# Two matrix products of a fused attention and MLP kernel rewritten as seven block products for eight

## The chip, the cores and the metric

The kernel runs on one core of a Trainium2 chip. A core has TensorE (PE in the profile; PEld are its weight loads), VectorE (DVE), ScalarE (ACT), GpSimd (POOL) and SyncE (SP, which issues most transfers). The metric is the device time of one execution in microseconds; the profile's span runs from the first to the last instruction.

## The reference, cut to what matters

```python
# attention: 2 batches, 12 heads, 448 tokens, head size 64, causal
scores = scale * np.matmul(q, k.transpose(0, 1, 3, 2))
scores = np.where(mask, -1000000000.0, scores)
scores = scores - np.max(scores, axis=-1, keepdims=True)
attn = np.exp(scores)
attn = attn / (np.sum(attn, axis=-1, keepdims=True) + 1e-09)
x = np.matmul(attn, v)            # as 896 tokens x 768
# first MLP: w_in 768 x 2048, w_out 2048 x 768
r = np.maximum(x @ w_in, 0.0)
x = (r * r) @ w_out
# second MLP: w1, w2, w3, w_o 768 x 768
h = np.maximum(np.maximum(x @ w1, x @ w2), x @ w3)
out = h @ w_o
```

q, k and v are float32, the weights arrive as float64 (the loads take them as four int16 a number).

## The kernel before, in words

Every engine runs its instructions in the order in which the function writes them (`manual_schedule`); semaphores hold an instruction until its operands are there.

**Attention.** Heads go in pairs (12 pairs, `Pair`). A pair has seven score units: `s` (TensorE, L246), `m` (VectorE: mask, minimum and a copy to SBUF, L257), `e` (ScalarE: exponential with its sum, L266), `r` (VectorE: reciprocal, L273, L274), `n` (GpSimd: multiply, L278), `g` (TensorE: transposes, L286), `h` (copies out of PSUM, L310, group 0 on VectorE, the others on ScalarE), `w` (TensorE: times v, L319), and `xh`, `xl`: the result of the pair split into a high part (ScalarE, `act_hi`, L128) and the rest (VectorE, `dve_lo`, L131). `ORDER` is a list, written out, of all these steps with the pair's number behind the point. It also has some first products of w_in (`p`, `a`, `b`), which fill TensorE.

**Products.** Each float32 product is three passes of TensorE: high x high, high x low, low x high. A weight block of 768 x 128 goes through five steps: `load` (SyncE queue, two buffers), `cast` (ScalarE, L159), `join` (VectorE, L166), `high_part` (ScalarE), `low_part` (VectorE). `decode` puts the steps of the next blocks and the evacuation of the last accumulators in turn. For w_in, `group` (L356) multiplies a block with both batches of x, 6 contraction blocks x 3 passes x 2 batches of 448 columns; then relu on ScalarE (L382), the product of relu and value on VectorE (L386), and the split into gh and gl. w_out takes 16 contraction blocks for each of 6 output blocks. w1, w2 and w3 run as w_in does, with maxima on VectorE (L586).

**Last product.** The product with w_o (L615) is already made from seven block products for eight, 384 columns each; its sums are made on VectorE (L553) and its results leave through L683 and L684.

Of the kernel before, what the change touches and what calls it, by code (L numbers as in the profile page):

```python
# [60 lines left out]
def tile_attention_moe_moe(  # L61
# [23 lines left out]


# [40 lines left out]
    def act_hi(hi, src):  # L127
        nc.scalar.copy(hi, src)  # L128

    def dve_lo(lo, src, hi):  # L130
        nc.vector.tensor_tensor(out=lo, in0=src, in1=hi.bitcast(F32), op=ALU.subtract)  # L131


    class Weight:

        def __init__(self, pool, w, k0, nk, c0, n, tag, bufs=None):
            self.pool, self.src, self.tag, self.bufs = pool, w, tag, bufs  # L140
# [606 lines left out]
```

## Time and profile before

| | |
|---|---|
| runs | 492.59, 492.68, 494.93 us (median 492.68) |
| profiled execution | 493.42 us, its span 491.5 us |
| TensorE busy | 486.4 us, 2587 matmuls |
| VectorE busy | 254.5 us, 530 instructions |
| ScalarE busy | 231.5 us, 451 instructions |
| GpSimd busy | 45.4 us, 99 instructions |
| granted TensorE clock | 1.00 throughout |

A busy share is an average over stages with different limits, and a matmul's end is modelled in the records, so neighbouring matmuls overlap. What a stage is limited by is read from the chain of waits and from the busy time of each engine in that stretch.

### The profile page before, as it was taken

The page shows a single profiled execution, that of the slowest core. Times are in us where ns is not written, and L with a number is a line of the kernel's source. Part 1 is how long each engine was busy: PE and PEld are TensorE (multiplying, and loading weights), DVE is VectorE, ACT ScalarE, POOL GpSimd, SP SyncE. Part 2 cuts the span into 40 slices and gives each one's busy share as a digit, 9 for nine tenths or more (in the row PEclk, how much of TensorE's full clock was granted, in tenths as well). Part 3 has the DMA queues.
Part 4 walks back from the last instruction along what each step waited for, and adds up shares of the span by engine and source line. Part 5 has one row for each costly group of instructions (what it writes and reads, how often), then busy time and mean ns, then how long its engine had stood idle before and what let it go on. Part 6 is the DMA issues. An engine that isn't in the chain of part 4 may idle for free.

```text
span 491.5 us, 6744 instructions
## 1 busy us (share of the span) xinstructions
PE 486.4 (99%) x2587; PEld 429.5 (87%) x2587; DVE 254.5 (52%) x530; ACT 231.5 (47%) x451; POOL 45.4 (9%) x99
## 2 busy tenths in 40 slices
PE   9999999999999999999999999999999999999997
PEld 5666667999999999999999999999999999999996
DVE  5877766555455456514315224226463638564942
ACT  6999996555455455414214224133443515332800
POOL 5655633000000000000000000000000000000000
PEclk9999999999999999999999999999999999999999
DMA  6553414252442441525225144133454435210022
GB/s 203 165 192 119 148 45 125 75 176 77 126 124 75 125 128 49 165 65 171 83 89 162 43 139 132 61 128 122 136 167 153 144 116 191 74 56 1 32 99 94
DMA packets 47615, 56.26 MB, mean 114 GB/s; under 512 B 1760, under 2 KB 43872, under 8 KB 47584
## 3 DMA queue, kind: packets, MB, share of 16 engines
q1 hardware_dynamic: 47296, 55.61, 35.6%
q8 instruction: 20, 0.33, 0.3%
q10 hardware_dynamic: 288, 0.23, 0.1%
q14 instruction: 11, 0.09, 0.1%
HBM read 53.08 MB, written 2.75 MB: 114 GB/s over the span
## 4 chain that ended last, share of the span: by engine, by line
PE 98%; DVE 1%; POOL 1%; issue 0%
PE ps L356 75%; PE ps L615 8%; PE ps L246 6%; PE ps L286 4%; PE ps L319 4%; POOL pr L278 1%; PE ps L465 1%; DVE pr L257 0%; DVE xl L131 0%; DVE wd L683 0%; DVE warm L463 0%; DVE st L273 0%; DVE st L274 0%; DVE st L257 0%
## 5 line engine op out<-in xcount | busy, mean ns | idle before, releaser
L128 ACT CAST wh<-wd 128x768 fp32r<-128x768 f32 (+1 forms) x52 | 42.2, 811 | 62.9 <-DVE wd L166 62.9
L159 ACT CAST up<-wr 128x768 f16<-128x768 bf16 (+1 forms) x58 | 60.7, 1046 | 9.8 <-DMA wr<-in_moe_w_out 5.0
L131 DVE TENSOR_TENSOR wl<-wd,wh 128x768 fp32r<-128x768 f32 (+1 forms) x52 | 48.1, 925 | 29.8 <-ACT wh L128 29.8
L356 PE MATMUL ps<-yh,wh 128*128 128x448 f32 x216 | 61.6, 366 | 0.0
L356 PE MATMUL ps<-yh,wl 128*128 128x448 f32 x216 | 61.6, 366 | 0.0
L356 PE MATMUL ps<-yl,wh 128*128 128x448 f32 x216 | 61.5, 366 | 0.0
L166 DVE SCALAR_TENSOR_TENSOR wd<-wr,up 128x768 int32<-128x768 int32 (+1 forms) x58 | 53.9, 929 | 9.1 <-ACT up L159 9.0
L356 PE MATMUL ps<-xh,wh 128*128 128x448 f32 x192 | 55.9, 367 | 0.0
L356 PE MATMUL ps<-xh,wl 128*128 128x448 f32 x192 | 55.7, 366 | 0.0
L356 PE MATMUL ps<-xl,wh 128*128 128x448 f32 x192 | 55.7, 366 | 0.0
L356 PE MATMUL ps<-gl,wh 128*128 128x448 f32 x192 | 54.5, 365 | 0.0
L356 PE MATMUL ps<-gh,wh 128*128 128x448 f32 x192 | 54.5, 365 | 0.0
L356 PE MATMUL ps<-gh,wl 128*128 128x448 f32 x192 | 54.5, 365 | 0.0
L266 ACT ACTIVATE pr<-pr,st 128x128 f32<-128x128 f32 (+3 forms) x84 | 44.0, 528 | 6.5 <-DVE st L257 6.5
L278 POOL TENSOR_SCALAR pr<-pr,st 128x128 f32<-128x128 f32 (+3 forms) x84 | 41.6, 513 | 32.2 <-DVE st L274 13.5
L386 DVE SCALAR_TENSOR_TENSOR r<-ps,r 128x448 f32<-128x448 f32 x32 | 18.6, 620 | 49.6 <-ACT r L382 49.6
L356 PEld LDWEIGHTS ps<-yl,wh 128*128 128x128 f32 x216 | 40.6, 188 | 3.5
L356 PEld LDWEIGHTS ps<-yh,wl 128*128 128x128 f32 x216 | 40.6, 188 | 3.5
L356 PEld LDWEIGHTS ps<-yh,wh 128*128 128x128 f32 x216 | 40.6, 188 | 3.5
L257 DVE CUSTOM_DVE_ANT_0 pr<-ps,mask 128x128 f32<-128x128 f32 (+3 forms) x84 | 34.5, 449 | 10.3 <-PE ps L246 9.4
L356 PEld LDWEIGHTS ps<-xl,wh 128*128 128x128 f32 x192 | 36.1, 188 | 3.1
L356 PEld LDWEIGHTS ps<-xh,wl 128*128 128x128 f32 x192 | 36.1, 188 | 3.1
(123 smaller groups left out, 620.5 us busy)
## 6 DMA issues: line engine op xcount, KB each, us to landing
wr<-in_moe_w_out SPq DMA_DIRECT2D x18, 768.0 KB, 4.3
wr<-in_moe_w SPq DMA_DIRECT2D x18, 768.0 KB, 4.3
wr<-in_moe_w_in SPq DMA_DIRECT2D x16, 768.0 KB, 4.7
v<-in_v SPq DMA_DIRECT2D x12, 256.0 KB, 3.4
wr<-in_moe_w_out SPq DMA_DIRECT2D x6, 512.0 KB, 3.7
q<-in_q SPq DMA_DIRECT2D x11, 256.0 KB, 2.9
k<-in_k SPq DMA_DIRECT2D x11, 224.0 KB, 3.7
out<-wd SPq DMA_DIRECT2D x9, 192.0 KB, 1.8
```

The lines of the kernel that those rows point to most:

```text
L128: nc.scalar.copy(hi, src)
L131: nc.vector.tensor_tensor(out=lo, in0=src, in1=hi.bitcast(F32), op=ALU.subtract)
L159: nc.scalar.copy(self.up.bitcast(FH)[:, :, 1::2], self.top)
L166: nc.vector.scalar_tensor_tensor(out=self.t.bitcast(I32), in0=self.rest, scalar=13, in1=self.up.bitcast(I32), op0=ALU.logical_shift_right, ...
L246: nc.tensor.matmul(sc[:, :keys[w]], self.n["q"][r, w // 2 * P:(w // 2 + 1) * P], self.n["k"][r, :keys[w]], start=True, stop=True,)
L257: nc.vector.tensor_tensor_reduce(out=self.pr[:, offs[u]:offs[u] + n], in0=self.sc[u][:, :n], in1=mask[:, mask.shape[1] - n:], scale=-SCALE ...
L266: nc.scalar.activation(sl, sl, ACTF.Exp, bias=self.st[:, 0, u:u + 1], scale=-1.0, accum_out=self.st[:, 1, u:u + 1],)
L278: nc.gpsimd.tensor_scalar(sl, sl, self.st[:, 2, u:u + 1], 1.0, op0=ALU.mult, op1=ALU.mult)
L286: nc.tensor.transpose(pt[:, i], self.pr[:, offs[u] + kc * P:offs[u] + (kc + 1) * P], shared["ident"])
L319: nc.tensor.matmul(self.pv[r, kc * P:], self.n["v"][:, kc, r], self.ph[:, h, at], start=kc == 0, stop=kc == NK - 1,)
L356: nc.tensor.matmul(acc[i], ww[:, cs], xx[:, tk], start=first and a == 0 and n == 0, stop=last and a == len(kcs) - 1 and n == 2,)
L615: nc.tensor.matmul(acc, x, w, start=start and a == 0 and i == 0, stop=stop and a == len(parts) - 1 and i == 2, skip_group_check=more,)
```

## The change

The products with w_in and with w1 to w3 are made from quarters. Of x (896 tokens x 768) a11 is batch 0 with the first three contraction blocks, a12 batch 0 with the last three, a21 and a22 the same of batch 1. Of two column blocks of a weight, each is cut into halves of three contraction blocks. Seven products M1 to M7 of sums of quarters take the place of eight. The sums of x are s3 = a11 - a21, s2 = a22 - s3, s1 = s2 + a11 and s4 = a12 - s2; they are made per contraction block on VectorE and each is split into high and low parts. The sums of weights are four subtractions on VectorE per pair of column blocks. M1, M6, M7 and M4 accumulate in one PSUM bank, and what it holds after M1, M6 and M7 is copied out by ScalarE (`keep`) and added on VectorE to the other two banks.

The head pairs are taken in the order that gives the four quarters of one contraction block together: pair i has batch i%2 and heads i//4 + 3*(i%4//2). `ORDER` is new, and steps of different pairs are interleaved singly. It holds four products (slots 0 to 3, steps `u`), their weight work (`k0` to `k26`) and the sums of x (`d`, `1h` to `4l`). Each later product is a slot; behind its matmuls stand the evacuation of the slot before, the weight work planned for it (`plan`, `LEAD` = 3 slots ahead) and extras, such as the conversion of g to gh and gl. SBUF is handed out as 47 equal units (`Units`). GpSimd's clearing of two `up` tiles becomes VectorE's of one, put first. w_out and the last product keep their number of matmuls; the last one's sums and conversions are spread over the end of the w1 to w3 stage and its own.

```diff
-FILL, EARLY = 1, 2
+LEAD = 3
+RING = 5
+OWN, MORE = 29, 18
+BESIDE = 4
 ORDER = """
...
+w3.9 k14 r2.11 n2.11 h0'.10 e5.11 h2.10 u0.2 d3.9 h1.10 k16 k17 u1.0 n3.11 e6.11 g1.11 n0.11 w0.10
+r0.11 k23 w1.10 n6.11 3h.9 k20 2l.7 n1.11 w2.10 w3.10 h1.11 u3.0 u1.1 k18 n4.11 xf.10 xh.10 k19
+n5.11 g2.11 g0.11 k21 xl.10 h2.11 h0'.11 g3.11 u1.2 h3.11 v1.0 w0.11 k24 w1.11 k25 k26 w2.11 w3.11
+d2.11 2h.11 d4.11 d1.11 4h.11 2l.11 u3.1 xh.11 4l.11 1h.11 1l.11 xl.11 u2.1 u3.2 3l.9 u2.2 v2.0
...
+    class Quarter:
...
+        def hi(self):
+            self.t = wp.tile([P, 2, KH, P], FR, tag="q", name="wq", bufs=RING)
+            act_hi(self.t[:, 0, :self.nk], self.src())
+
+        def lo(self):
+            dve_lo(self.t[:, 1, :self.nk], self.src(), self.t[:, 0, :self.nk])
+            self.of().used()
...
+        t1 = Op(sums(0, b12, b11, ka, kb), [a, b])
+        t2 = Op(sums(1, b22, of(0), k0, kb), [t1])
+        t3 = Op(sums(2, b22, b12, kb), [b])
+        t4 = Op(sums(3, b21, of(1), k0, ka), [t2])
...
-        ups.append(pool.tile([P, KDM * P], F32, name="up1", bufs=1))
-        for t in ups:
-            nc.gpsimd.memset(t, 0.0)
...
+        def x_full(self, copy):
+            t = full[self.kind] = s_tile()
+            copy(t, self.pv)
...
+        def sum_of(self, n):
+            a, b, op = {
+                "s3": (full.get(0), self.pv, SUB), "s2": (self.pv, full.get("s3"), SUB),
+                "s1": (full.get("s2"), full.get(0), ADD), "s4": (full.get(2), full.get("s2"), SUB),
+            }[n]
+            t = full[n] = s_tile()
+            dve(t, a, b, op)
+
+        def sum_hi(self, n, copy):
+            self.t[n] = operand(n, self.c)
+            copy(self.t[n][:, 0], full[n])
+
+        def sum_lo(self, n):
+            dve_lo(self.t[n][:, 1], full[n], self.t[n][:, 0])
...
+    PASSES = ((0, 0), (0, 1), (1, 0))
+    OPERANDS = dict(M1="a11", M2="a12", M6="s2", M5="s1", M7="s3", M4="a22", M3="s4")
...
+            self.acc = {n: self.b for n in OPERANDS} | dict(M5=self.c, M3=self.c, M2=self.d)
...
+        def run(self, n, ks=range(KH)):
+            for i in ks:
+                for e, (ew, ex) in enumerate(PASSES):
                     nc.tensor.matmul(
...
+                        self.acc[n], self.q[n].t[:, ew, i], X[OPERANDS[n]][i][:, ex],
+                        start=n in ("M1", "M2", "M5") and i == 0 and e == 0,
+                        stop=i == KH - 1 and e == 2, skip_group_check=True,
                     )
...
+        def keep(self, n):
+            self.s[n] = s_tile()
+            nc.scalar.copy(self.s[n], self.b)
...
+    def pipelined(groups):
+        a, b, *rest = groups
+        s = [(a, "M1"), (b, "M1"), (a, "M2"), (b, "M2"), (a, "M6"), (a, "M5"), (a, "M7")]
+        s += [(b, "M6"), (a, "M4"), (b, "M5"), (a, "M3"), (b, "M7")]
+        for x in rest:
+            s += [(x, "M1"), (b, "M4"), (x, "M2"), (b, "M3"), (x, "M6"), (x, "M5"), (x, "M7")]
+            b = x
+        return [x.slot(n) for x, n in s], [b.slot("M4"), b.slot("M3")]
...
+    for n, e in enumerate(slots):
+        for x in e.quarter.needs if e.quarter else ():
+            plan(x, n - LEAD - 1 - (first_third <= n < first_third + 8))
...
+    def beside(n):
+        before, late = way_out(n)
+        if n in urgent:
+            before = before + [urgent[n]]
+        for step in before + weight_steps(n) + late + extra.get(n, []):
+            step()
+        units.settle()
...
+    order = [(x6, "M4"), (x7, "M2"), (x6, "M3"), (x7, "M6"), (x7, "M5"), (x7, "M7"), (0, 0), (0, 0)]
+    order += [(x7, "M4"), (0, KH), (0, KH), (x7, "M3"), (0, 2 * KH), (0, 2 * KH), (0, 3 * KH), (0, 3 * KH)]
+    for f, where in enumerate(order):
+        also(where, lambda f=f: convert(f))
...
+    def y_last(i):
+        u, (a12, a22) = y[i][0], shared["y"]
+        shared["s2"] = s2 = s_tile()
+        hi_of("a12", i, a12)
+        lo_of("a12", i, a12)
+        dve(s2, a22, u[:, 1], SUB)
+        hi_of("s2", i, s2)
+        dve(u[:, 0], s2, u[:, 0], ADD)
+        hi_of("s1", i, u[:, 0])
+        lo_of("s2", i, s2)
+
+    def y_end(i):
+        u, (a12, a22) = y[i][0], shared["y"]
+        s4 = s_tile()
+        dve(s4, a12, shared["s2"], SUB)
+        hi_of("a22", i, a22)
+        lo_of("s1", i, u[:, 0])
+        hi_of("s4", i, s4)
+        lo_of("a22", i, a22)
+        lo_of("s4", i, s4)
+        units.give(y[i][1])
...
+    urgent[first_third] = lambda: y_last(KH - 1)
+    also(first_third, lambda: y_end(KH - 1))
...
+    nc.vector.memset(up, 0.0)
...
+    for n in range(BESIDE, len(slots)):
+        slots[n].run()
+        beside(n)
```

## Rows read from the trace of the kernel before

**Rows 1.** The page's engine table, TensorE to GpSimd.

```profile
PE 486.4 (99%) x2587; PEld 429.5 (87%) x2587; DVE 254.5 (52%) x530; ACT 231.5 (47%) x451; POOL 45.4 (9%) x99
```

**Rows 2.** Chain of waits in order of time: start us, us, what.

```profile
70.64 0.41 DVE pr L257
...
76.38 1.09 PE ps L286 x8
...
80.38 3.66 PE ps L356 x18
84.04 1.88 PE ps L319 x16
85.92 362.95 PE ps L356 x1782
448.87 39.20 PE ps L615 x225
...
488.09 0.56 DVE wd L683
```

**Rows 3.** Busy us by stretch: length, PE, PEld, DVE, ACT, POOL, clock, DMA.

```profile
0.00:86.00 86.00, 84.39 (x581) 55.85 (x582) 62.26 (x270) 73.59 (x235) 45.44 (x99) 1.00 0.47 143
5.00:80.00 75.00, 74.58 (x529) 48.00 (x528) 57.82 (x262) 69.65 (x229) 41.60 (x84) 1.00 0.45 139
...
170.00:190.00 20.00, 20.00 (x100) 18.41 (x99) 11.94 (x15) 11.01 (x15) 0.00 (x0) 1.00 0.29 90
```

**Rows 4.** Groups by form: shape, count, busy us, mean ns, idle before.

```profile
L159 ACT CAST up<-wr 128x768 f16<-128x768 bf16 x52 | 56.0, 1077 | 9.8 <-DMA wr<-in_moe_w_out 5.0 <-DMA wr<-in_moe_w 4.4
...
L166 DVE SCALAR_TENSOR_TENSOR wd<-wr,up 128x768 int32<-128x768 int32 x52 | 49.8, 957 | 9.1 <-ACT up L159 9.0
...
L386 DVE SCALAR_TENSOR_TENSOR r<-ps,r 128x448 f32<-128x448 f32 x32 | 18.6, 620 | 49.6 <-ACT r L382 49.6
L131 DVE TENSOR_TENSOR gl<-r,gh 128x896 fp32r<-128x896 f32 x15 | 16.4, 1093 | 2.5 <-ACT gh L128 0.9
...
L382 ACT ACTIVATE r<-ps 128x448 f32<-128x448 f32 x32 | 15.8, 543 | 44.5 <-PE ps L356 44.5
...
L131 DVE TENSOR_TENSOR wsum<-wd,wsum 128x384 fp32r<-128x384 f32 x8 | 4.0, 549 | 0.0
...
L128 ACT CAST wsum<-wd 128x384 fp32r<-128x384 f32 x8 | 3.6, 510 | 0.0
```

**Rows 5.** Timeline of VectorE in the last stage: start us, us, instructions.

```profile
455.18 1.35 DVE L131 TENSOR_TENSOR halves<-zs,halves 128x1152 fp32r<-128x1152 f32 x1
456.45 1.49 DVE L131 TENSOR_TENSOR wsums<-wd,wsums 128x384 fp32r<-128x384 f32 x3
457.86 1.35 DVE L131 TENSOR_TENSOR halves<-zs,halves 128x1152 fp32r<-128x1152 f32 x1
```

**Rows 6.** Timeline of ScalarE in the last stage.

```profile
457.34 0.51 ACT L128 CAST wsums<-wd 128x384 fp32r<-128x384 f32 x1
457.75 0.93 ACT L128 CAST wsum<-wd 128x384 fp32r<-128x384 f32 x2
458.58 1.15 ACT L128 CAST halves<-zs 128x1152 fp32r<-128x1152 f32 x1
```

**Rows 7.** Timeline of the first five microseconds.

```profile
3.10 1.41 POOL L125 MEMSET up<- 128x768 f32 x2
...
4.57 0.29 DVE L257 CUSTOM_DVE_ANT_0 pr<-ps,mask 128x128 f32<-128x128 f32 x1 [3.44 <-PE ps L246]
...
4.90 0.40 ACT L266 ACTIVATE pr<-pr,st 128x128 f32<-128x128 f32 x1 [1.97 <-DVE st L257]
```

**Rows 8.** Line 166 up to 100 us: ns min/median/max, first and last start.

```profile
L166 DVE SCALAR_TENSOR_TENSOR wd<-wr,up x5: 948/949/1183, 75.9 to 99.3; 128x768 int32<-128x768 int32 x5
```

**Rows 9.** Timeline of GpSimd, 72 to 78 us.

```profile
73.44 5.06 POOL L278 TENSOR_SCALAR pr<-pr,st 128x256 f32<-128x256 f32 x9 [2.55 <-DVE st L273]
```

**Rows 10.** ScalarE's waits, 4.9 to 80 us: us in total, times, longest.

```profile
ACT pr L266 <- DVE st L257: 6.5, 12, 2.0
```

More of the change, by code (lines that the diff above doesn't have):

```diff
@@ L200, in next_acc @@
-    def next_acc():
-        turn["acc"] += 2
-        return [e[:, :S] for e in ps[(turn["acc"] - 2) % 8:][:2]]
     keys = [(u // 2 + 1) * P for u in range(2 * NQ)] + [S]
@@ new lines, in tile_attention_moe_moe, with zf, wf @@
+    for e in outs[1:]:
+        slots += e
+    head, tail = pipelined(thirds)
+    first_third = len(slots)
+    slots += head + [None, tail[0], None, tail[1], None]
+    TH, n2 = NTT // 2, DM // 2
+    first, second, last = slice(0, TH * P), slice(TH * P, 2 * TH * P), slice(2 * TH * P, NT)
+    left, right = slice(0, n2), slice(n2, DM)
+    z1, z2, zr, wo, half, piece = {}, {}, {}, {}, {}, {}
+    def zf(f):
+        return z[f][0].rearrange("p b s -> p (b s)")
+    def wf(f):
+        return blocks_o[f].t[:, 0]
@@ L676, in tile_attention_moe_moe, with weight_steps @@
-    ways = iter((early * (TH + 2))[:TH + 2] + late * TH)
-    def way_out(t, cs, acc, other=None):
-        o = next(ways)
-        if other is None:
-            nc.scalar.copy(o, acc)
-        else:
-            nc.vector.tensor_tensor(out=o, in0=acc, in1=other, op=ALU.add)
-        nc.sync.dma_start(out=out[rows(t), cs], in_=o)
-    for acc, cs in zip(rest, (left, right)):
-        way_out(NTT - 1, cs, acc)
+    def weight_steps(n):
+        mine = [op for op in ops if when[op] == n]
+        r = [op.step for op in mine if op.block]
+        if 0 <= n + LEAD < len(slots) and slots[n + LEAD].quarter:
+            r += [slots[n + LEAD].quarter.hi, slots[n + LEAD].quarter.lo]
+        r += [op.step for op in mine if not op.block and op.needs]
+        return r + [op.step for op in mine if not op.needs]
@@ new lines, in tile_attention_moe_moe @@
+    more = ctx.enter_context(tc.tile_pool(name="more", bufs=1))
+    units.add(more, MORE, "m")
+    for e in range(2):
+        todo[f"v{BESIDE - 1}.{e}"]()
+    for n in range(BESIDE, len(slots)):
+        slots[n].run()
+        beside(n)
+    before, late = way_out(len(slots))
+    for step in before + late:
+        step()
+    t_1(0)
+    t_3(0)
+    t_2(KH)
+    z_lower(KH + 1)
+    z_lower(KH + 2)
+    for f in range(KF2):
+        x = zr["t"][0][:, f] if f < KH else None
+        x = [x[:, 0], x[:, 1]] if f < KH else [e[0][:, last] for e in z2[f]]
+        for e, (ex, ew) in enumerate(((0, 0), (0, 1), (1, 0))):
+            for acc, cs in zip(rest, (left, right)):
+                nc.tensor.matmul(
+                    acc, x[ex], wo[f][ew][0][:, cs], start=f == 0 and e == 0,
+                    stop=f == KF2 - 1 and e == 2, skip_group_check=True,
+                )
@@ L695, in tile_attention_moe_moe @@
-        for o, a, b in ((u, acc[1], u), (v, acc[2], u)):
-            nc.vector.tensor_tensor(out=o, in0=a, in1=b, op=ALU.add)
-        way_out(TH + t, right, acc[0], v)
-        product(acc[0], quarter(z22, t4, t), False, more=True)
-        way_out(t, right, acc[3], v)
-        way_out(TH + t, left, acc[0], u)
+        product(cc[t], halves("s1", t), pieces("t1"))
+    s_half("s3", KH - 1)
+    units.give(z[KH - 1][1])
+    units.settle()
+    for i in range(KH):
+        t_piece("t3", i)
+    for t in range(TH):
+        product(bb[t], halves("s3", t), pieces("t3"), False)
@@ L703 @@
+    for t in range(TH):
+        finish("s2", t, cc[t], t, right)
 _INS = [
```

921 lines of the change are left out of this document (553 added, 368 removed).

## Prediction

> **What bounds the kernel now.** I read the page's engine table first. TensorE is at 99%, but matmul records overlap and their ends are modelled, so that figure alone proves little [rows 1]. The chain of waits is the second view: from 85.92 us on it is TensorE and nothing else, 1782 matmuls in 362.95 us, which is 0.2037 us a matmul of 448 columns, then 225 of 384 columns in 39.20 us, 0.1742 us each [rows 2]. The reader is to see that a chain without a single step on another engine means that matmuls taken out there are time taken out, as long as the other engines still deliver. Eighteen matmuls with a new weight block each also take 3.66 us, 0.203 us apiece [rows 2], so the new order, in which no two neighbours share their weights, has the same price.
>
> The table by stage, the third view, says what the other engines have left. Between 170 and 190 us VectorE is busy 11.94 us of 20 and ScalarE 11.01 [rows 3]: room. Before 86 us it is the other way round: from 5 to 80 us ScalarE is busy 69.65 us of 75, VectorE 57.82, while TensorE's weight loads fill 48.00 [rows 3]. The attention stage is held by ScalarE almost as much as by TensorE, though the chain names TensorE.
>
> **What matmuls go.** w_in has 16 column blocks, 6 contraction blocks, 3 passes and 2 batches: 576 matmuls. Eight groups of 7 products with 3 x 3 matmuls are 504. w1 to w3 go from 648 to 567. So 153 matmuls leave, 153 x 0.2037 = 31.2 us. The w_out and last-matrix products keep their counts (576; 225). Were nothing else touched, the span would be 491.5 - 31.2 = 460.3 us.
>
> **What an operation on VectorE and ScalarE costs.** In the list by form a 384-wide subtraction lasts 549 ns [rows 4], but in a row three of them occupy 456.45 to 457.86 us, 0.47 us each, and a 1152-wide one 1.27 us of its 1.35 [rows 5]. Records overlap by 0.08 us on VectorE. On ScalarE two 384-wide casts occupy 457.75 to 458.58 us, 0.415 us each against 510 ns listed [rows 4, 6]: 0.10 us overlap. I price by spacing and keep durations as the upper bound. So VectorE: 0.47 (384 wide), 0.54 (448, listed 620), 0.88 (decode join of 768, listed 957), 1.01 (896, listed 1093). ScalarE: 0.415 (384), 0.44 (448, listed 543), 0.98 (decode cast, listed 1077) [rows 4]. A 448-wide cast from SBUF is not in those rows; between 0.44 and the 0.46 that 64 columns more than 384 would give, 0.46.
>
> **The attention stage.** The mark I use is the end of the last head pair's weighted sum (w3.11), 85.92 us before [rows 2]. ScalarE up to there: 73.59 us busy [rows 3], of which 1.28 is the table load at the start; without the operations that the change touches (11 hi casts, two weight blocks, one relu and its cast: 9.0) 63.3 us remain for exponentials and copies. The change puts in, before the mark: 6 full copies (xf) and 8 hi casts from PSUM at 0.44, 9 hi casts of Strassen sums at 0.46, 4 decode casts at 0.98, 7 quarter casts at 0.415 and one keep at 0.44: 6.2 + 4.1 + 3.9 + 2.9 + 0.4 = 17.5 us. Sum 80.8 us. ScalarE begins with the first exponential at 4.90 us [rows 7]; that becomes 5.5, since the clearing of `up`, two memsets of 1.41 us on GpSimd [rows 7], becomes one on VectorE ahead of the warm-up's memset, some 0.7 us. So ScalarE cannot reach the mark before 86.3 us.
>
> VectorE by the same count: 62.26 us busy to the mark [rows 3], 51.9 of it untouched; added 16 lo parts and 9 sums at 0.54, 4 joins, 7 quarter lo parts, 5 weight sums: 13.5 + 3.5 + 3.3 + 2.4 = 22.7. It starts at 4.57 now [rows 7], 5.2 then, and could be there at 79.9. TensorE: 85.92 less the stall of 70.64 to 76.38 us, in which the chain runs through VectorE and GpSimd [rows 2], plus 6 more matmuls before the mark (24 for 18), plus 0.7: 82.1 us. ScalarE is therefore what sets the mark. It also waited: 75 - 69.65 = 5.35 us between 5 and 80 [rows 3]. I keep that idle time, no less because two engines are now nearly full, no more because the finer order gives the matmuls of four products to fill with. Bounds 0 and 10.7; taken 5.35: mark at 91.6 us.
>
> Here a rule decides which engine to count. The Trainium skill (Perfetto Trace Analysis, Identifying the Most-Contended Engine) calls matmul busy time a bad metric and has weight-load busy time looked at instead. The trace agrees: weight loads are busy 48.00 of 75 us there against 18.41 of 20 at 170 us [rows 3]. Counting TensorE as the page shows it would give a mark of 82.1 and 9.5 us less in all.
>
> Another speaks against the change. One decode join took 1183 ns where the median is 949 [rows 8], and it lies inside a run of nine GpSimd multiplications [rows 9]. The Trainium skill (GPSIMD Engine Reference, Key points) says that GpSimd shares its SBUF interfaces with VectorE and collides with its instructions of two SBUF inputs. By that, 24 more such instructions before the mark at 0.234 us are 5.6 us, VectorE reaches 85.5 without waiting, and if all of it reached ScalarE the sum would be 474. I leave it in the range.
>
> **After the mark.** 1647 matmuls of 448 columns remain in all, 24 of them before the mark: 1623 x 0.2037 = 330.6 us. The last matrix takes 39.2, its last sum 0.6, the way out of the last tile 491.5 - 488.65 = 2.85 us [rows 2].
>
> What hides the vector work, group by group: VectorE per pair of w_in columns has 2 joins, 7 lo parts, 4 weight sums, 3 additions, 3 squares and 1 relu product: 1.76 + 3.3 + 1.9 + 1.6 + 1.6 + 0.5 = 10.7 us against 63 x 0.2037 = 12.8 on TensorE. ScalarE: 2 casts, 7 hi parts, 3 keeps, 1 relu, 6.6 us. For w1 to w3 nine groups make 90 us, and the pieces of the last matrix beside them some 17: 107 against 120. Both fit. In the last stage 49 operations of 384 and two of 896 columns are 25 us against 198 matmuls, 34.5 us, most of them a product ahead; I charge nothing.
>
> Two places do not fit. Where the last two w_in groups end, 16 conversions of g come in: 16.2 us, with 10 evacuation operations 5.4, 12 lo parts 5.6, sums and joins 5.3 make 32.5 us against 29.3 us of matmuls; the conversions lead their use by one slot (2.4 to 3.7 us), so 0 to 3 us show, taken 1.5. At the first w1 products the four late sums and their lo parts (y_last, y_end) are 4.3 us at once, with seven slots' slack of 2.1 against them and four slots until M6 needs them: 0 to 2, taken 0.5.
>
> SP's queue: q, k and v are still requested behind s0 and w0, a weight block right behind the join that frees its buffer, two blocks per 12.8 us in two buffers as now; stores leave at the end as now. I charge nothing for it.
>
> **Sum.** 91.6 + 330.6 + 39.2 + 0.6 + 2.85 + 2.0 = 466.9 us span. The profiled execution had 493.42 around 491.5, 1.9 more; the median of the runs is 492.68, 0.7 less than that execution. So 466.9 + 1.9 - 0.7 = 468 us, 5.0% faster.
>
> **Rivals.**
> *All of it comes back* (chance 0.15): ScalarE waits for nothing more, the two places are covered: 468 - 5.35 - 2 = 460.7, up to 463. For it: the fine interleaving and the filling products; against: ScalarE had idle time in the present order with less to do.
> *VectorE becomes the bound* (0.21): if operations cost their durations because each waits for another engine's result, the conversions need 35.8 us against 29.3 (6.5 lost), w1 to w3 123 against 120 and 3 at their start, the last stage about 4 for its first quarters: 16 less the 2 counted, 482; half of that, 475. For it: most lo parts follow a ScalarE cast; against: casts are planned three slots ahead.
> *ScalarE's queue stops on the new sums* (0.09): each of the 12 hi casts of a Strassen sum stands in ScalarE's order behind a VectorE sum that itself waits for the head pair's last matmul, and the next exponentials stand behind it. The longest wait of that kind now is 2.0 us [rows 10]. Twelve of these would be 24 us, 492: no change; from 2.3 us each on the kernel is slower than 495. Against it: the sum comes at least one exponential ahead of its cast nearly everywhere in the written order.
> My forecast, 463 to 473, has 0.55.
>
> **Range and chances.** 460 to 480 holds the forecast, most of the first rival, half to two thirds of the second, and leaves the third out. A measurement of this kernel tells some 0.5% from no change (its runs spread from 492.59 to 494.93). Faster 0.91, within 0.5% 0.04, slower 0.05, the last two from the third rival.
>
> **What would show it.** Right: the chain after the mark again TensorE alone at 0.204 us a matmul, 1623 and 225 of them; the mark at 90 to 93; ScalarE over 90% busy before it. Wrong at the mark: it lies before 87 (ScalarE was overpriced) or beyond 97, with ScalarE's waits naming VectorE sums. Wrong behind it: chain pieces on VectorE at the end of w_in, at the first w1 products or in the last stage, or VectorE above 95% busy there; or matmuls of the quarters spaced by more than 0.204 us though nothing waits.

## The result, and the profile after

The changed kernel takes 469.64 us (median of four runs, 469.27 to 473.84) against 493.02 for the kernel before on the same chip (492.59 to 494.93): a ratio of 0.9538, 95% interval 0.9478 to 0.9598. The prediction was 468.0, between 460 and 480. The execution profiled took 469.29 us, its span 467.5.

The engine table of the kernel after answers to [rows 1]. VectorE's busy time rises by 105 us and ScalarE's by 55, TensorE's falls by 26; TensorE's share hardly moves, and says nothing here.

```profile
PE 460.4 (98%) x2434; PEld 398.4 (85%) x2434; DVE 359.6 (77%) x796; ACT 286.8 (61%) x619; POOL 50.0 (11%) x97
```

The chain of waits of the kernel after, in order of time, answers to [rows 2] (start us, us, what):

```profile
59.40 0.87 ACT ph L408 x2
60.27 0.98 ACT pr L365 x4
...
70.61 0.48 ACT ph L408
71.10 0.04 issue
71.13 0.94 POOL pr L377 x2
...
85.09 0.59 ACT ph L408
85.68 0.98 ACT up L163
86.66 0.02 issue
86.68 0.96 DVE wd L168
...
87.76 0.19 DVE st L373
...
88.13 1.21 POOL pr L377
89.34 1.03 POOLq L1121
90.37 1.14 POOL pr L377 x2
...
91.56 1.20 PE ps L385 x9
...
93.37 1.88 PE ps L416 x16
95.25 94.03 PE ps L498 x462
189.28 3.65 PE ps L626 x18
192.93 1.99 PE ps L498 x9
...
198.57 1.82 PE ps L498 x9
200.39 109.44 PE ps L626 x540
309.83 111.26 PE ps L498 x549
421.10 1.56 PE ps L751 x9
...
435.74 28.33 PE ps L751 x162
464.07 0.02 issue
464.09 0.56 DVE s L123
```

The reader is to see two halves. From 95.25 us, the mark, the chain is TensorE alone: 1848 matmuls in 368.82 us, where [rows 2] have 402.15. Ahead of the mark it leaves TensorE twice: from 59.11 to 72.12 us it is ScalarE nearly throughout, with two multiplications of GpSimd (0.94) at the end, and from 85.07 to 91.56 us it goes through ScalarE, VectorE and GpSimd. The mark lies 9.33 us later than before. So 33.3 us were saved behind the mark and 9.3 given back ahead of it: 24.0, the difference of the two spans.

The table by stage of the kernel after (columns as in [rows 3]) shows both halves:

```profile
5.50:95.25 89.75, 88.05 (x571) 51.78 (x569) 74.56 (x293) 81.17 (x251) 47.47 (x84) 1.00 0.45 143
190.00:210.00 20.00, 20.00 (x100) 18.30 (x99) 19.82 (x29) 17.20 (x26) 0.00 (x0) 1.00 0.34 106
330.00:350.00 20.00, 20.00 (x100) 18.54 (x99) 17.38 (x33) 10.93 (x19) 0.00 (x0) 1.00 0.38 125
```

While g is converted, VectorE is busy 19.82 us of 20 and TensorE still hardly waits (0.17 us, below); in w1 to w3 VectorE has 17.38. The cover is thin and holds.

### The profile page after: what moved, and what is told of

Its sections match the earlier page's. It is cut to its first block, busy times and chain, and to the rows that moved or that the text cites. A ratio compares the mean times of both kernels' runs of the same rounds, so it can differ in the third digit from the quotient of the medians.

```text
span 467.5 us, 6967 instructions
## 1 busy us (share of the span) xinstructions
PE 460.4 (98%) x2434; PEld 398.4 (85%) x2434; DVE 359.6 (77%) x796; ACT 286.8 (61%) x619; POOL 50.0 (11%) x97
## 4 chain that ended last, share of the span: by engine, by line
PE 95%; ACT 3%; POOL 1%; DVE 1%; issue 0%; POOLq 0%
PE ps L498 46%; PE ps L626 25%; PE ps L751 7%; PE ps L346 6%; PE ps L385 5%; PE ps L416 4%; PE ps L1013 1%; ACT pr L365 1%; POOL pr L377 1%; ACT ph L408 1%; PE ps L961 1%; ACT up L163 0%; POOLq L1121 0%; DVE wd L168 0%; ACT wq L113 0%
## 5 line engine op out<-in xcount | busy, mean ns | idle before, releaser
L498 PE MATMUL ps<-s,wq 128*128 128x448 f32 x612 | 127.4, 365 | 0.0
L498 PEld LDWEIGHTS ps<-s,wq 128*128 128x128 f32 x612 | 114.9, 188 | 9.3 <-ACT s L508 0.3
L498 PE MATMUL ps<-a,wq 128*128 128x448 f32 x459 | 97.4, 366 | 0.0
L626 PE MATMUL ps<-gh,wq 128*128 128x448 f32 x384 | 93.9, 365 | 0.0
L498 PEld LDWEIGHTS ps<-a,wq 128*128 128x128 f32 x459 | 85.7, 188 | 7.1 <-ACT s L508 0.3
L116 DVE TENSOR_TENSOR wq<-wd,wq 128x384 fp32r<-128x384 f32 (+1 forms) x87 | 46.6, 540 | 46.4 <-ACT wq L113 42.3
L626 PEld LDWEIGHTS ps<-gh,wq 128*128 128x128 f32 x384 | 72.1, 188 | 5.7
L626 PE MATMUL ps<-gl,wq 128*128 128x448 f32 x192 | 54.5, 365 | 0.0
L377 POOL TENSOR_SCALAR pr<-pr,st 128x256 f32<-128x256 f32 (+3 forms) x84 | 47.5, 583 | 40.7 <-DVE st L373 24.2
L365 ACT ACTIVATE pr<-pr,st 128x384 f32<-128x384 f32 (+3 forms) x84 | 44.2, 532 | 4.6 <-DVE st L357 4.5
(104 smaller groups left out, 490.7 us busy)
```

Source lines behind the costliest of these rows:

```text
L365: nc.scalar.activation(sl, sl, ACTF.Exp, bias=self.st[:, 0, u:u + 1], scale=-1.0, accum_out=self.st[:, 1, u:u + 1],)
L377: engine.tensor_scalar(sl, sl, self.st[:, 2, u:u + 1], 1.0, op0=ALU.mult, op1=ALU.mult)
L498: nc.tensor.matmul(self.acc[n], self.q[n].t[:, ew, i], X[OPERANDS[n]][i][:, ex], start=n in ("M1", "M2", "M5") and i == 0 and e == 0, stop ...
L626: nc.tensor.matmul(acc[b], quarter.t[:, ew, f - k0], (gh, gl)[ex][f][0][:, b], start=f == 0 and e == 0, stop=f == KFF - 1 and e == 2, skip ...
```

## The experiments

Each run of the first eleven is one execution with a profile; they are compared by spans and marks, against 467.5 and 95.25 of the changed kernel. Two things have to be known for that. The 462 matmuls of w_in behind the mark take 94.01 to 94.05 us in some executions and 95.69 to 95.70 in others, with the same instructions, so a span can be 1.7 us off for no reason of the edit. The mark moves by itself too: three of the runs change nothing ahead of it (one product more, one product fewer, quarters later), and their marks are 95.37, 95.30 and 96.26. The difference is there within the first thirteen microseconds, at ScalarE's first copy of transposed scores out of PSUM; here it is in the changed kernel and in the run with the later quarters (start us, us):

```profile
11.58 0.56 ACT L408 COPY ph<-ps 128x512 f32<-128x512 f32 x1
12.64 0.59 ACT L409 COPY ph<-ps 128x512 f32<-128x512 f32 x1
```

From the start of that copy to the mark these four executions take 83.67, 83.55, 83.62 and 83.62 us. So the distance from the first copy to the mark is the safest measure of what an edit does to the attention stage. What makes the first copy come at 11.5 to 12.6 us was not found.

**One product more in w1 to w3.** Line 496 of the changed kernel, for M3 of each group:

```diff
-            for i in ks:
+            for i in [*ks, *ks] if n == "M3" and isinstance(self, Third) else ks:
```

> M3 of every w1 to w3 group is run twice (9 groups x 9 matmuls, 81 more), which is the number of matmuls of eight products for eight; the values of that quarter are then not the reference's. Theory (behind the mark TensorE alone sets the time): 81 x 0.2033 = 16.5 us more, span 484.0 against 467.5, chain again TensorE alone. Rival (VectorE, 87 to 93% busy in that stage, already shares the bound): clearly less, 8 us or under, since the longer matmuls would partly fill time in which TensorE waits anyway.

The span is 485.5, 18.0 longer. The chain of this run (start us, us, what), beside 94.03 and 111.26 above:

```profile
95.37 95.70 PE ps L498 x462
...
311.63 125.86 PE ps L498 x621
```

1.67 us of the 18.0 lie in w_in's stretch; the other 16.3 are what 81 x 0.2027 gives (111.26 / 549 = 0.2027), within 0.1. A matmul put in costs its full price.

**One product fewer.** The same line, with M3 left out:

```diff
+            for i in [] if n == "M3" and isinstance(self, Third) else ks:
```

> M3 of every w1 to w3 group is left out (81 matmuls fewer), everything VectorE and ScalarE do stays; one quarter of each of these products is then not the reference's. TensorE has 54 x 0.2033 = 11.0 us a group against 10.7 us that I counted for VectorE by spacing (plus its share of the last matrix). Theory (spacing is the right price, VectorE just fits under the present 12.8 us but hardly under 11.0): 16.5 us would be taken out, 9 to 14 arrive, span 453 to 458, and VectorE reaches 97% or more in that stage with chain pieces on it. Rival A (VectorE has ample room): the full 16.5, span 451. Rival B (VectorE already bounds the stage): under 5 us, span over 462.

The span is 461.4: 81 matmuls fewer gave 6.1 us of 16.5, less than the 9 to 14 of the theory and more than rival B allowed. Some 2.2 us of what is missing are not the edit's: the 540 matmuls of w_out took 111.60 us here and 109.44 in the changed kernel. From the end of that stretch to the end of the last product it is 145.8 us here against 154.2, 8.4 less, half of what was taken out. The table by stage of this run:

```profile
330.00:350.00 20.00, 20.00 (x99) 18.15 (x98) 19.60 (x37) 13.03 (x23) 0.00 (x0) 1.00 0.49 163
350.00:370.00 20.00, 19.19 (x94) 17.18 (x93) 19.60 (x38) 14.66 (x28) 0.00 (x0) 1.00 0.65 211
```

VectorE is at 19.60 of 20 in the stage where the changed kernel has 17.38, and the chain goes through its instructions, twice also through the transfer of a weight block that waits for a VectorE join to free its buffer (4.27 and 4.46 us). The two runs together say: at seven products TensorE sets the pace of w1 to w3, at six VectorE does, with those transfers behind its joins. The prediction's 107 us of vector work against 120 put the crossing at about 6.2 products (7 x 107 / 120); by these two runs it lies at about 6.5 (an estimate: 7 - 8.4 / 16.5).

**Quarters one slot ahead instead of three**, behind the attention stage:

```diff
-        if 0 <= n + LEAD < len(slots) and slots[n + LEAD].quarter:
-            r += [slots[n + LEAD].quarter.hi, slots[n + LEAD].quarter.lo]
+        at_ = n + (LEAD if n < BESIDE else LATE)
+        if 0 <= at_ < len(slots) and slots[at_].quarter and (n < BESIDE or at_ >= BESIDE + LEAD):
+            r += [slots[at_].quarter.hi, slots[at_].quarter.lo]
```

with `LATE = 1`.

> After the attention stage the high and low part of a quarter are made one slot ahead of its product instead of three; nothing else moves. Theory (the two places that I charged 2 us for are hidden by the three slots of lead): without that cover the chain ScalarE cast to VectorE subtraction to weight load shows where VectorE is over 95% busy, at the conversions of g, the first w1 products and the end: 5 to 25 us more, span 473 to 493. Rival (VectorE has room everywhere, the lead is not needed): 467 to 469.

The span is 489.5, 22 us longer with the same instructions. The waits of TensorE's weight loads in this run (us in total, times, longest):

```profile
PEld ps L499 <- DVE wq L117: 16.4, 33, 2.1
```

The changed kernel, from the mark to the end, waits for 0.6 us:

```profile
PEld ps L498 <- ACT s L508: 0.6, 2, 0.3
```

Not all of the 22 us are the edit's. 1.0 us lies ahead of the mark, where nothing was changed. Its w_out matmuls are spaced by 0.2067 us where the changed kernel has 0.2027, which is some 2.3 us in 576 of them:

```profile
209.89 91.57 PE ps L627 x443
```

Were all three long stretches spaced as in the last run below, 6 us of the 22 would be spacing, so the edit is worth 15 us or more (an estimate from these numbers). At least some three fifths of the gain of 24 us hang on the three slots of lead.

**What sets the mark: ScalarE's work.** The full copies of six pair results are made twice (ScalarE's busy time up to the mark becomes 84.03 us for 81.17):

```diff
             t = full[self.kind] = s_tile()
             copy(t, self.pv)
+            copy(t, self.pv)
```

> Each of the six full copies xf of a head pair's result is made twice by ScalarE (6 x 0.44 = 2.6 us more ScalarE work before the mark). The mark is at 95.25 us now. Theory (ScalarE's work sets the mark): 97.5 to 98, span 470. Rival (the wait of the last head pair's multiplications on GpSimd behind VectorE's joins sets it; ScalarE has 8.6 us idle there): mark within 0.7 us of 95.25, span 467 to 468.3.

The mark comes 1.57 us later, at 96.82, with the first copy where it was (11.57): about half of what was added, not all of it. Neither side is right.

**VectorE's work.** The sums of x are made twice (VectorE's busy time up to the mark becomes 79.47 us for 74.56, 4.9 more):

```diff
             t = full[n] = s_tile()
             dve(t, a, b, op)
+            dve(t, a, b, op)
```

> Each of the twelve sums of x (d1 to d4) is made twice by VectorE: 9 before the mark, 4.9 us more VectorE work there, 3 right behind it. Theory (ScalarE's work sets the mark, VectorE's fits beside it): mark at 95.3 to 96.5, span 467.5 to 469. Rival (VectorE's queue, in which reciprocals stand behind sums and joins, sets it): mark at 98.5 to 100.5, span 471 to 473.

The mark comes 4.8 us later, at 100.0, and the span is 473.2. The first copy is 0.5 us late here (12.11), ahead of any doubled sum, so 4.3 us are the edit's. Here the rival was right: VectorE's instructions, put where the sums stand, come through nearly whole.

**ScalarE relieved.** The twelve casts of those sums go to GpSimd (ScalarE's busy time up to the mark becomes 77.50 us for 81.17):

```diff
             self.t[n] = operand(n, self.c)
-            copy(self.t[n][:, 0], full[n])
+            nc.gpsimd.tensor_copy(self.t[n][:, 0], full[n])
```

> The twelve hi casts of the sums of x (1h to 4h) go from ScalarE to GpSimd; 9 x 0.46 = 4.1 us less on ScalarE before the mark, some 9 x 0.65 = 5.9 us more on GpSimd, which is busy 47.5 us of 90. Theory (ScalarE's work sets the mark): mark 2 to 4 us earlier, 91.3 to 93.3, span 463.5 to 465.5. Rival (the multiplications on GpSimd set the end of the attention stage): mark at 95 to 99, since the casts stand among the multiplications in GpSimd's queue.

The mark is later, not earlier: 99.40. The list by form of GpSimd in this run (count, busy us, mean ns, idle before), and in a second fence GpSimd's waits:

```profile
L442 POOL CAST s<-s 128x448 fp32r<-128x448 f32 x12 | 8.9, 751 | 8.7 <-DVE s L123 8.7
```

```profile
POOL s L442 <- DVE s L123: 8.7, 5, 4.5
```

GpSimd stands still behind the sums for 8.7 us, up to 4.5 at a time, and the last normalisations come late. This is the rival of the prediction that a queue stops on the new sums, on another engine. The 4.15 us have two more parts. The first copy is 0.74 us late (12.32). And TensorE, which stood still for 0.82 and 0.88 us behind GpSimd's multiplications between 72 and 75 us, then has a granted clock of 0.50, the lower of its two levels (1.2 of 2.4 GHz), from 76 to 79 us:

```profile
76.00:79.00 3.00, 3.00 (x14) 1.69 (x14) 2.85 (x12) 1.33 (x5) 1.81 (x4) 0.50 0.03 5
```

The steps that the chain has there take 4.77 us (75.83 to 80.60) and 3.25 in the changed kernel (73.62 to 76.87), 1.5 more. The run takes work from ScalarE and holds GpSimd up at once, so it does not tell what less work on ScalarE alone would bring.

**The last pair's reciprocal earlier.** Two weight steps are taken behind the last exponential and reciprocal:

```diff
-d3.9 h1.10 k16 k17 u1.0 n3.11 e6.11 g1.11 n0.11 w0.10 r0.11 k23
+d3.9 h1.10 u1.0 n3.11 e6.11 g1.11 n0.11 w0.10 r0.11 k16 k17 k23
```

> In the written order the decode cast and join k16 and k17 move from ahead of the last exponential and the last reciprocal (e6.11, r0.11) to behind them. Theory for the last ten microseconds of the attention stage (the last reciprocal at 87.56 waits for a join that waits for a cast, 0.98 + 0.96 us): mark 1.0 to 1.9 us earlier, 93.3 to 94.3, span 465.6 to 466.6. Rival (all of ScalarE's work has to be done before the mark in any order): mark at 95 to 95.6, span 467 to 468.

The reciprocal comes at 86.71 us instead of 87.76, the mark at 95.07: 0.18 earlier, or 0.42 counted from the first copy (11.82). GpSimd's timeline in this run shows where the rest went; in the changed kernel the last four multiplications take 3.37 us from 88.13:

```profile
87.08 4.24 POOL L377 TENSOR_SCALAR pr<-pr,st 128x448 f32<-128x448 f32 x4 [1.02 <-DVE st L373]
```

They start 1.05 us earlier and take 0.87 us longer.

**The clearing of `up` back on GpSimd.**

```diff
-    nc.vector.memset(up, 0.0)
...
         constants(att)
+        nc.gpsimd.memset(up, 0.0)
```

> The clearing of up goes back from VectorE's first instruction to GpSimd, behind its masks. Theory (the start is passed on, since an engine that is full from there on starts earlier): first exponential 0.7 to 0.8 us earlier, mark 0.5 to 0.8 us earlier, span 466.7 to 467.0. Rival (it is swallowed by waits later): same mark, span 467.3 to 468.

The first exponential starts at 4.94 us instead of 5.71, as forecast, and the mark is at 95.17, 0.08 earlier. The first copy starts at 11.54 instead of 11.58: the earlier start is swallowed within the first twelve microseconds already.

**VectorE relieved.** The 36 additions of 1e-9 ahead of the reciprocals are left out, in the changed kernel and in the kernel before:

```diff
-            nc.vector.tensor_scalar_add(st[:, 2, cs], st[:, 1, cs], 1.0e-9)
-            nc.vector.reciprocal(st[:, 2, cs], st[:, 2, cs])
+            nc.vector.reciprocal(st[:, 2, cs], st[:, 1, cs])
```

> The addition of 1e-9 ahead of each of the 36 reciprocals is left out (a sum of exponentials is at least 1, to which 1e-9 adds nothing in float32): 36 VectorE operations fewer, 6.7 us busy before the mark, ScalarE and GpSimd as they are. The earlier runs gave +4.8 us at the mark for 4.9 us more of VectorE and +1.6 for 2.6 more of ScalarE. New theory (VectorE's queue sets the mark, since its reciprocals and sums stand one behind the other): mark 4 to 6 us earlier, 89 to 91, span 461.5 to 464. Rival (ScalarE's work or GpSimd's multiplications set it): mark 93 to 95.3, span 465.5 to 467.5.

> The same 36 additions left out of the kernel before. VectorE is busy 57.8 of 75 us there. Theory (VectorE became the limit of the attention stage only with the change): the mark at 85.92 moves by less than 2 us, span 489.5 to 491.5. Rival (reciprocals are on the chain in either kernel): 3 us or more, span under 488.5.

In both kernels the mark comes 0.81 us earlier (94.44 from 95.25, 85.11 from 85.92), though VectorE's busy time up to the mark fell by 6.1 and 6.5 us. The theory for the changed kernel, by then that VectorE alone sets the mark, falls as well. For the kernel before the forecast came out, but its ground, that only the changed kernel has VectorE as its limit, is not borne out where both move alike. The spans are 466.7 and 490.7.

**The last pair's multiplications on VectorE**, three of them:

```diff
-k23 w1.10 n6.11 3h.9
+k23 w1.10 n6'.11 3h.9
...
-u1.1 k18 n4.11 xf.10
+u1.1 k18 n4'.11 xf.10
...
-k19 n5.11 g2.11
+k19 n5'.11 g2.11
```

> The last three multiplications of the last head pair (n4, n5, n6 of pair 11) go from GpSimd, where the last four took 3.37 us, to VectorE. Theory (GpSimd's end is on the chain, and its multiplications last 1.0 to 1.2 us there because VectorE works on two SBUF inputs at the same time): mark 0.8 to 2 us earlier, 93.3 to 94.4, span 465.6 to 466.7. Rival (VectorE's queue is as full as GpSimd's at that point): within 0.5 us of 95.25, or later.

The mark is at 95.33, as the rival has it. But the first copy is 0.75 us late here (12.33), and from it to the mark it is 83.00 us for 83.67: the edit took out 0.67 us, a little less than the theory asked for. The GpSimd pieces at the end of the chain are gone, and from 72.86 us to the mark it names TensorE alone.

**TensorE's steps in rows of one kind.** The last run takes the version without the additions and moves 16 names of the order (the expectation counts 15) in 13 moves, of which three are shown:

```diff
-xf.2 xh.2 g3.4 h2.4 n3.4 xl.2 s6.6 g0.4
+xf.2 xh.2 h2.4 n3.4 xl.2 s6.6 g3.4 g0.4
...
-g3.9 m4.10 s2.10 1h.7 d4.7 h1.9 m3.10 n1.10 e4.10 g0.9
+m4.10 s2.10 1h.7 d4.7 h1.9 m3.10 n1.10 e4.10 g3.9 g0.9
...
-w0.8 m2.10 w1.8 s2.11 h0'.9 e5.10 4h.7 w2.8
+m2.10 s2.11 h0'.9 e5.10 4h.7 w0.8 w1.8 w2.8
```

> The 36 additions of 1e-9 are left out as in the run that left them out alone (mark 94.44), and 18 TensorE steps of the written-out order are put directly ahead of the next step of their own kind (13 moves, 15 names; single transposes, weighted sums and scores), so that TensorE changes between scores, transposes and weighted sums 69 times up to the last weighted sum instead of 87 times (65 in the kernel before). Nothing else is changed. Theory: the mark is set by TensorE's own steps, which cost more one by one than in rows (the chain's pieces show 4 transposes alone at 0.59 us and 8 together at 1.02, so about 0.15 to 0.2 us for each change); 18 fewer give 2.7 to 3.6 us, so the mark falls to 90.8 to 91.7 us and the span to 463 to 464. Rival: the changes of kind cost nothing of their own, TensorE only waits for what the other engines deliver; then the mark stays within 0.5 us of 94.44, or comes later because the moved steps are later, and the span stays at 466.7 or more.

The mark is at 95.76, 1.32 us later than without the moves: the theory falls. The table by stage for this run and, in the second fence, for the one that only leaves the additions out:

```profile
5.50:95.76 90.26, 86.54 (x571) 52.21 (x569) 67.76 (x257) 81.27 (x251) 46.76 (x84) 1.00 0.45 142
```

```profile
5.50:94.44 88.94, 87.37 (x573) 51.43 (x569) 68.47 (x257) 80.64 (x251) 47.25 (x84) 1.00 0.46 144
```

TensorE's matmuls are busy 0.83 us less in a stretch 1.32 us longer, its weight loads 0.78 us more; whether rows of one kind cost less is not shown by that. That the moved steps come later would explain the mark, but the chain of this run has a piece that no other run's has ahead of the mark, the transfer of a weight block (start us, us; the second line is from ScalarE's timeline):

```profile
57.05 8.57 DMA wr<-in_moe_w_in
```

```profile
65.70 1.07 ACT L163 CAST up<-wr 128x768 f16<-128x768 bf16 x1 [0.91 <-DMA wr<-in_moe_w_in]
```

ScalarE stands still for 0.91 us until it lands; in the run that only leaves the additions out the longest transfer of such a block between 40 and 70 us took 7.0 us, and no ScalarE wait for one is in its list. So up to 0.9 of the 1.32 us may be that transfer, and one profile does not tell whether the new order delays it. Timed in six runs this version takes 473.44 us (470.08 to 475.98), 0.9548 of the kernel before, interval 0.9511 to 0.9585: no different from the change itself. Its profiled execution has the slower spacing in all three long stretches (95.69 us for 462, 111.60 for 540, 113.46 for 549), which makes some 6 us. No version that was run is measurably better than the changed kernel; the one without the additions has the shortest span of those with seven products, 466.7, by one execution.

## Why the prediction came true, and which terms were off

**Behind the mark.** The sum had 330.6 + 39.2 us of matmuls and 2.0 of stalls, 371.8; the chain shows 368.82. The count was right (1623 and 225) and the price too (0.2027 to 0.2035 us a matmul, 0.2037 assumed). The run with one product more shows that a matmul there costs its price; the one with one fewer that this holds for seven products and not for six, and the one with a shorter lead that it holds only while the quarters are made early.

**The stalls.** 1.5 us for the conversions of g and 0.5 for the first w1 products were charged. The chain has nine matmuls at 1.99 us there that take 1.82 later on: 0.17 us in all. At 19.82 of 20 us VectorE does not fall behind far enough to be seen: instructions that follow each other overlap, as priced, and the slots of lead absorb the rest, which the run with one slot of lead bears out. The rival in which VectorE becomes the bound did not come about, but the run with six products shows it begin within one product of the present load. By the prediction's own signs of being wrong, VectorE above 95% busy at the end of w_in was one, and it is at 99% there; the chain stays with TensorE all the same, so the sign was badly chosen.

**The mark.** 91.6 was forecast, 95.25 came. The work terms held: ScalarE 81.17 us busy from 5.5 us to the mark (80.8 predicted), VectorE 74.56 (51.9 + 22.7 = 74.6 predicted). The term that failed is ScalarE's idle time, put at 5.35 us and measured 89.75 - 81.17 = 8.58. The step that failed is where it was read: from the stretch of 5 to 80 us [rows 3], while the sum runs to the mark. The table by stage of the kernel before, over the full stretch and its two parts, has the rest:

```profile
4.90:85.92 81.02, 80.60 (x565) 52.63 (x563) 61.57 (x267) 72.28 (x233) 41.60 (x84) 1.00 0.46 142
4.90:80.00 75.10, 74.68 (x529) 48.08 (x528) 57.92 (x262) 69.75 (x229) 41.60 (x84) 1.00 0.45 139
80.00:85.92 5.92, 5.92 (x39) 4.55 (x37) 3.65 (x6) 2.53 (x4) 0.00 (x0) 1.00 0.63 189
```

ScalarE is idle 81.02 - 72.28 = 8.74 us up to the mark of before, 3.39 of them in the last six, while the last pair's steps follow one another from engine to engine. The kernel after has the same two parts:

```profile
5.50:80.50 75.00, 73.54 (x474) 41.71 (x473) 63.29 (x267) 70.23 (x223) 40.82 (x75) 1.00 0.51 161
80.50:95.25 14.75, 14.51 (x100) 10.06 (x98) 11.27 (x29) 10.94 (x29) 6.65 (x9) 1.00 0.18 55
```

4.77 us in the body and 3.81 at the end. With 8.74 in its place the sum gives 5.5 + 80.8 + 8.74 = 95.0. That idle time was kept as a whole is luck in part: before, 4.6 us of ScalarE's waits up to 80 us were for VectorE's score results; after, it waits 3.3 us for TensorE's transposes and 1.7 for those results, and no run here shows why the two come to the same. The 3.65 us at the mark were made up for by the stalls (1.8 less) and the spacing (1.1 less). Two misses of opposite sign that have nothing to do with each other: that the total is nearer than its terms is luck. The mark itself, 95.25, lies in neither the 90 to 93 that were to show the prediction right nor beyond the 97 that were to show it wrong.

**"ScalarE is therefore what sets the mark"** is borne out in part at most. The chain after does go through ScalarE for some 12 us ahead of 72 us. The marks, with the first copy that each is counted from:

| run | first copy, us | mark, us | distance, us | against 83.67 |
|---|---|---|---|---|
| changed kernel | 11.58 | 95.25 | 83.67 | |
| ScalarE's copies twice, 2.86 us more | 11.57 | 96.82 | 85.25 | +1.58 |
| VectorE's sums twice, 4.9 us more | 12.11 | 100.04 | 87.93 | +4.26 |
| casts to GpSimd | 12.32 | 99.40 | 87.08 | +3.41 |
| reciprocal earlier | 11.82 | 95.07 | 83.25 | -0.42 |
| clearing on GpSimd | 11.54 | 95.17 | 83.63 | -0.04 |
| additions left out, 6.1 us less | 11.54 | 94.44 | 82.90 | -0.77 |
| multiplications to VectorE | 12.33 | 95.33 | 83.00 | -0.67 |
| additions left out, rows of one kind | 11.52 | 95.76 | 84.24 | +0.57 |

Work added to VectorE came through nearly whole, to ScalarE about half; relief brought 0.8 us at most. The runs agree with a stage in which each engine waits for the next in a written order, so that any of them can lengthen it and none alone shorten it by much. That is argued from them together, with one profile of each; no single wait was found that sets the mark. No run takes work from ScalarE without giving it to an engine on the chain, and an order made anew for the relieved engines was not tried: that ScalarE holds the stage as a whole is not ruled out.

**The rivals.** That ScalarE stops on the twelve sums: its waits for them are 1.2 us in two, the longest 1.0, where twelve of 2.0 were allowed. The 2.0 was misread: it is the wait ahead of the very first exponential ([rows 7] has it with 1.97), and the longest of that kind behind it is 0.8 us in the kernel before. ScalarE's waits in the kernel after, behind the first exponential and up to the mark, answer to [rows 10]:

```profile
ACT ph L408 <- PE ps L385: 3.3, 5, 1.5
ACT pr L365 <- DVE st L357: 1.7, 5, 0.6
ACT s L442 <- DVE s L123: 1.2, 2, 1.0
```

All of it coming back fails at the idle time.

Two rules were cited. For the one that calls matmul busy time a bad metric (the Trainium skill, Perfetto Trace Analysis, Identifying the Most-Contended Engine) the runs speak: up to the mark TensorE is busy 88.05 us of 89.75 by its matmuls and 51.78 by its weight loads, and over the variants with the same TensorE steps and a granted clock of 1.00 in the stage the first figure goes from 86.54 to 89.73 and the second only from 51.43 to 52.21.

The other, that GpSimd and VectorE's instructions with two SBUF inputs collide (the Trainium skill, GPSIMD Engine Reference, Key points), fits what both engines show, at a lower price than the one feared. VectorE's low parts of the sums have two SBUF inputs; ahead of the mark, where GpSimd works, they last up to 1.04 us, behind it 0.63 at most (ns min/median/max, first and last start):

```profile
L116 DVE TENSOR_TENSOR s<-s,s x8: 595/618/1040, 34.4 to 88.3; 128x448 fp32r<-128x448 f32 x8
L116 DVE TENSOR_TENSOR s<-s,s x4: 616/618/626, 97.0 to 99.2; 128x448 fp32r<-128x448 f32 x4
```

Their mean ahead of the mark is 731 ns, so the eight cost 0.9 us more than 619 each. The four joins there take 975 ns in the mean against 950 behind it. 24 instructions at 0.234 us, 5.6 us, had been priced. GpSimd's multiplications became longer as well. The list by form of the kernel after:

```profile
L377 POOL TENSOR_SCALAR pr<-pr,st 128x448 f32<-128x448 f32 x12 | 8.6, 715 | 6.4 <-DVE st L373 6.0 <-ACT pr L365 0.4
```

It was 642 ns a multiplication before. Shared interfaces would explain both; no run here separates them from other causes.

## What to carry to other kernels

When the chain of waits names one engine for a long stretch, work taken out there comes back at the price of its spacing, as far as the next engine's busy time in that same stretch: here half a product of seven further, and only with the preparation three slots ahead. Idle time that is carried over from the profile of before has to be read over the very stretch that the sum covers, its end included, because the last steps of a pipeline leave idle time that its body does not show. Where several engines stand at 80 to 90% and hand work to each other, price what each change adds at half to nine tenths, and what it relieves at little (0.8 of 6.1 us here). Before a mark is compared between single executions, it has to be seen how far it moves in runs that change nothing ahead of it: 1.0 us here, of which 0.9 were gone when it was counted from a point behind the start.

## What was not expected of the hardware

The same 462 matmuls, with the same instructions ahead of them and no wait in the records, take 94.01 to 94.05 us in some executions and 95.69 to 95.70 in others, 0.2035 and 0.2071 us each, at a granted clock of 1.00 in those stretches. The w_out stretch does the same by itself: 109.44 us in most runs and 111.60 in two (one of them the run with six products, whose w_in stretch took 94.05). Where it takes 111.60 the starts of neighbouring matmuls are 206 or 207 ns apart throughout; where it takes 109.44 they are 198 to 207 ns apart, 202.7 in the mean. What decides it stays open; three such stretches are 6 us of a run here, as much as the spread of the six timed runs of the last version.

GpSimd's last four multiplications take 3.37 us in the changed kernel and 4.24 when they start a microsecond earlier. What else ran beside them differs between the two; which of it matters was not separated.
